# K S - V summed on TensorE and read by ScalarE in an attention's last chunks, low parts of the first weights on VectorE

## The chip, the core and the metric

One NeuronCore of a Trainium2 chip runs the whole program. The metric is device time in microseconds of one execution; lower is better.

## What is computed

The output of a delta-rule attention is the input of a rotating mixer, and that mixer's output goes through a normalised two-layer network. Shapes: batch 4, 8 heads, 768 tokens, head width 48, so 384 channels. Cut to what matters:

```python
for t in range(S):                                   # attention, per batch and head
    y[:, :, t] = q_t @ state
    v_old = k_t @ state                              # k_t is normalised
    state += beta_t * outer(k_t, v_t - v_old)
theta = x @ w_theta                                  # mixer on x = the attention's y
y = w_tok_r @ (x * cos(theta)) + w_tok_i @ (x * sin(theta))
u = x + y
u = u + relu(u @ w_ch)
xn = (u - mean) / sqrt(var + 1e-6) * g_ln            # network
out = u + relu(xn @ w_ch1) @ w_ch2
```

## The kernel before, in words

**Attention.** The tokens are cut into 24 chunks of 32. All 32 pairs of batch and head run side by side, as two halves h = 0, 1 of 16. Within a chunk the recurrence is solved with an inverse of a 32x32 triangle (PT, made for four chunks at a time on VectorE and POOL, the last one during chunk 18), so that only the state S runs from chunk to chunk. The loop body (L604 to L650) issues, in this order, for chunk c: R(0, c), which multiplies K with the state (L437, eight matmuls into the first half of the PSUM tile RW[0]) and has VectorE form Rs = V - K S (L440); S(1, c-1), the state update of the other half from the chunk before (L466) with two ScalarE copies into bds (L471); W(0, c), which multiplies PT with Rs (L452, second half of RW[0]) and has ScalarE copy the result into bdw in four pieces (L458); the output matmuls of chunk c-1 (L492), their ScalarE copy ys (L498) and four stores on SP's queue (L501); R(1, c); S(0, c); W(1, c); and the matmuls of q with the state (L481). Every engine starts its instructions in the order in which the program issues them to it. V is scaled by POOL two chunks ahead (L145). After the loop the last chunk's output matmuls follow (L651).

**Work of the next stage inside the attention.** At three places of each chunk, late(c, 0), late(c, 1) and late(c, 2), the program issues work of the mixer (L1149 to L1189). late(18, 2) sets constants (halfpi and magic, POOL memsets at L843 and L845, in memory that the inverse has just given back) and starts the weights' loads; late(20, 2) and late(21, 2) transpose the first two pieces of x (L870) and take them out as a high part xh (ScalarE, L879), a low part xl (VectorE, L883) and a copy u (ScalarE, L885, after xl); theta is a matmul (L897); angles make kk (ScalarE, L906) and nf (VectorE, L907); sines and cosines are ScalarE functions into the tile zf (L914, L915, L922), of which there is one buffer; turn multiplies zf with x on VectorE (L931) and copies it as the high part zh on ScalarE (L932); rest makes the low part zl on VectorE (L938).

**Weights.** Weights arrive as 64-bit floats in halves of 128x768 elements; there are two buffers for the raw halves, and the load of the next one waits on SP's queue until one is free. Weights.step, called at every late place from (19, 1) on, alternates between two actions. One finishes a half (parts, L800: ScalarE casts the high part at L813, then the low part is formed at L820, on POOL for the first two weights w0 and w1 and on VectorE from w2 on) and starts the next one (magnitude, L777, and clamp, L787 and L788, on VectorE), and then issues the next load. The other (low, L797 and L798, on VectorE) completes the bits and frees the raw buffer. The theta weights come first, then w0, w1 and w2 in two halves each. After the attention the same steps are issued by pump (L724), where the magnitude is ScalarE's (L781).

**Mixing.** Then 24 steps follow (L1239 to L1283), each with 36 matmuls (L957) that need one weight's high and low part and one zh and zl. Later stages are matmuls too (L1012, L1071, L1090).

Of the kernel before, what the change touches and what calls it, by code (L numbers as in the profile page):

```python
# [6 lines left out]
F32 = mybir.dt.float32  # L7
# [3 lines left out]
AF = mybir.ActivationFunctionType  # L11
ALU = mybir.AluOpType
# [4 lines left out]
NC = 24  # L17
# [72 lines left out]
        return False  # L90


def attention(ctx, tc, kq, ktok, vin, betai, maskin, x, psa, late=None):

    nc = tc.nc
    cst = ctx.enter_context(tc.tile_pool(name="a_cst", bufs=1))
# [334 lines left out]
    def R(h, c):  # L431
        if c == 0:
            return V[0][:, 4 * h:4 * h + 4, :]
        b = bds[h][c % 2]
        for g in range(2):
            for r in range(4):
                nc.tensor.matmul(RW[h][32 * r:32 * r + 32, 0, 2 * g:2 * g + 2, :], KQ[c][:, 0, 2 * h + g, r, :],  # L437
                                 b[:, 4 * g + r, :, :], start=True, stop=True)
        Rs = p2.tile([128, 4, D], F32, name=f"Rs{h}")
        nc.vector.tensor_tensor(out=Rs, in0=V[c][:, 4 * h:4 * h + 4, :], in1=RW[h][:, 0, :, :], op=ALU.subtract)  # L440
        return Rs

# [161 lines left out]
    for c in range(1, NC):  # L604
        s = c // 4
        step[0] = c
        load_kq(c + 11)
        load_v(c + 5)
        scale_v(c + 2)
        load_kt(c + 2)  # L610
        wa, wm, wq = Work(), Work(), Work()
        for n in {1: (9, 10), 2: (11, 12)}.get(c, (c + 10,)):
            if n < NC:
                a_work(wa, n)
        ym_work(wm, c - 1)
        yq_work(wq, c)
        R0 = R(0, c)
        budget = 2.3 if c >= 14 else 3.08
        if c % 4 == 1 and c > 1 and s + 1 < NS:
            while ("tg", s + 1) not in done:  # L620
                dv.step()
        dv.run(budget)
        if late:
            late(c, 0)
        wa.run((0.0 if c == 2 else 0.42) * wa.left())
        S(1, c - 1)
        W(0, c, R0)
        norms()
        wm.flush()
        R1 = R(1, c)  # L630
        dv.run(budget)
        if late:
            late(c, 1)
        if (c % 4 == 3 and s + 1 < NS) or c == 18:
            while s + 1 not in PT:
                if not dv.step():
                    norms()
        wa.flush()
        S(0, c)
        W(1, c, R1)  # L640
        norms()
        wq.flush()
        if c == 13:
            soon.close()
        if c == 18:
            mid.close()
        if c == 19:
            early.close()
        if late:
            late(c, 2)  # L650
    ym_work(pe, NC - 1)  # L651
    pe.flush()


def attn_inputs(q, k, v, beta):
# [173 lines left out]
class Mixer:  # L829
# [21 lines left out]
    def load_w(self, s, wtok, pool, wts, w=None):  # L851
        if pool:
            w = [pool.tile([128, 4, C], F32R, name=f"w{s}_{i}") for i in range(2)]
        self.W[s] = w
        for q in range(2):
            r = slice(2 * q, 2 * q + 2)
            wts.add(("w", s, q), wtok[s, q], lambda r=r: self.W[s][0][:, r], lambda r=r: self.W[s][1][:, r],
                    split=0 if s > 1 else None)

    def trans(self, i):  # L860

# [59 lines left out]
        zf = self.ZF  # L921
        nc.scalar.activation(out=zf[:, 0], in_=kk, func=AF.Sin, scale=-TWO_PI, bias=self.halfpi)  # L922

    def turn(self, i):
        nc = self.nc
        b, s = MIX[i]
        xs = self.x[s][:, b]
        zf = self.ZF
        zh = self.zp.tile([128, 2, C], F32R, name="zh")
        zl = self.zp.tile([128, 2, C], F32R, name="zl")  # L930
        nc.vector.tensor_tensor(out=zf, in0=zf, in1=bc(xs.unsqueeze(1), [128, 2, C]), op=ALU.mult)  # L931
        nc.scalar.copy(out=zh, in_=zf)  # L932
        self.Z[i] = zh, zl
        self.ZF2 = zf

# [189 lines left out]
def build(tc, a):  # L1125
# [8 lines left out]
    with tc.manual_schedule(), outer:  # L1134
# [10 lines left out]
        psa = outer.enter_context(tc.tile_pool(name="ps_a", bufs=2, space=PSUM, **R))  # L1145
        mx = Mixer(nc, x, psa, ident, uT)
        wts = Weights(nc, None, wide)

        def late(c, k):  # L1149
            if (c, k) == (13, 2):  # L1150
# [2 lines left out]
            if (c, k) == (18, 2):  # L1153
                nc.gpsimd.memset(ones.bitcast(F32), 1.0)
                nc.scalar.copy(out=ones, in_=ones.bitcast(F32))
                wts.st = ph1.enter_context(tc.tile_pool(name="st", bufs=1, **R))
                mx.load_theta(ph1, tc, a["wth"], wts)
                wts.load()
                nc.sync.dma_start(out=ident, in_=a["ident"])
                nc.sync.dma_start(out=g, in_=a["g"])  # L1160
            if (c, k) == (19, 2):
                mx.open(ph1, tc)
# [2 lines left out]
                wts.load()  # L1165
            if c > 19 or (c, k) == (19, 1):
                wts.step()
            if (c, k) == (16, 2):
                nc.scalar.activation(out=warm, in_=warm, func=AF.Sin)
            if (c, k) == (20, 2):  # L1170
# [7 lines left out]
            if (c, k) == (22, 2):  # L1178
                mx.cosines()
            if (c, k) == (22, 2):  # L1180
                mx.turn(0)
                mx.rest(0)
            if (c, k) == (23, 0):
                mx.theta(1)
                mx.angles(1)
            if (c, k) == (23, 1):
                mx.sines()
            if (c, k) == (23, 2):
                mx.cosines()  # L1189

        with ExitStack() as att:
            attention(att, tc, a["kq"], a["ktok"], a["vin"], a["betai"], a["mask"], x, psa, late)
        lp = outer.enter_context(tc.tile_pool(name="left", bufs=1))
        for b in range(1, 4):
            uT.append(lp.tile([128, KB, T], F32, name=f"u{b}"))
# [152 lines left out]
```

## Time and profile before

| | us |
|---|---|
| median of 3 runs | 785.29 |
| lowest of the runs | 783.65 |
| the profiled execution, in all | 786.73 |
| its span on the core | 784.8 |

| engine | busy us | share of the span |
|---|---|---|
| TensorE, matmul (PE) | 709.4 | 90% |
| TensorE, weight load (PEld) | 655.4 | 84% |
| VectorE (DVE) | 517.8 | 66% |
| ScalarE (ACT) | 356.9 | 45% |
| GpSimd (POOL) | 213.2 | 27% |

The profile's other views are used below: the chain that ended last, the busy time by stretch, groups of instructions by line with the idle time before them and what ended it, and the timeline of an engine. A releaser is the instruction whose semaphore came last. PEclk is the TensorE clock that was granted, as a share of full speed.

### The profile page before, as it was taken

The page shows a single profiled execution, that of the slowest core. Times are in us where ns is not written, and L with a number is a line of the kernel's source. Part 1 is how long each engine was busy: PE and PEld are TensorE (multiplying, and loading weights), DVE is VectorE, ACT ScalarE, POOL GpSimd, SP SyncE. Part 2 cuts the span into 40 slices and gives each one's busy share as a digit, 9 for nine tenths or more (in the row PEclk, how much of TensorE's full clock was granted, in tenths as well). Part 3 has the DMA queues.
Part 4 walks back from the last instruction along what each step waited for, and adds up shares of the span by engine and source line. Part 5 has one row for each costly group of instructions (what it writes and reads, how often), then busy time and mean ns, then how long its engine had stood idle before and what let it go on. Part 6 is the DMA issues. An engine that isn't in the chain of part 4 may idle for free.

```text
span 784.8 us, 18939 instructions
## 1 busy us (share of the span) xinstructions
PE 709.4 (90%) x7955; PEld 655.4 (84%) x7956; DVE 517.8 (66%) x875; ACT 356.9 (45%) x785; POOL 213.2 (27%) x234
## 2 busy tenths in 40 slices
PE   4577887777778999999997999999999999999997
PEld 3455555554468999999997999999999999999997
DVE  7987989986877888888876755435353534444342
ACT  2276776786775766654444433131322222131211
POOL 5854755744020001211111433113131221121120
PEclk8699999999989999999999999999999999999999
DMA  8975767234444223532432220000000000000000
GB/s 250 248 225 172 201 189 214 83 86 137 153 152 162 88 75 101 165 118 80 121 101 81 101 81 5 26 1 31 1 31 1 31 1 30 1 9 24 1 31 30
DMA packets 29716, 71.39 MB, mean 91 GB/s; under 512 B 4928, under 2 KB 17472, under 8 KB 29632
## 3 DMA queue, kind: packets, MB, share of 16 engines
q1 hardware_dynamic: 29632, 70.19, 29.0%
q8 instruction: 62, 1.02, 0.6%
q14 instruction: 22, 0.18, 0.1%
HBM read 56.02 MB, written 9.44 MB: 83 GB/s over the span
## 4 chain that ended last, share of the span: by engine, by line
PE 64%; DVE 15%; DMA 6%; ACT 6%; issue 5%; POOL 2%; SPq 1%; ACTq 0%; DVEq 0%; POOLq 0%
PE ph L1071 19%; PE acc L1090 19%; PE y L957 11%; PE pc L1012 5%; PE pth L897 3%; DMA bdk<-kq 3%; DVE prod L369 2%; ACT bdw L458 2%; DMA raw<-wtok 2%; PE py L492 1%; PE S L466 1%; PE pa L174 1%; DVE t L797 1%; PE RW L452 1%; DVE Ti L378 1%
## 5 line engine op out<-in xcount | busy, mean ns | idle before, releaser
L957 PE MATMUL y<-w,zh 128*128 128x384 f32 x576 | 154.8, 342 | 3.4 <-DVE u L966 2.4
L1090 PE MATMUL acc<-hh,f 128*128 128x384 f32 x576 | 147.0, 336 | 0.0
L1076 DVE SCALAR_TENSOR_TENSOR hl<-ph,hh 128x384 fp32r<-128x384 f32 x96 | 52.4, 553 | 114.5 <-ACT hh L1075 114.5
L1075 ACT ACTIVATE hh<-ph 128x384 fp32r<-128x384 f32 x96 | 46.7, 491 | 163.0 <-PE ph L1071 163.0
L1071 PE MATMUL ph<-xh,f 128*128 128x384 f32 x576 | 116.4, 337 | 0.4 <-DVE u L966 0.4
L957 PEld LDWEIGHTS y<-w,zh 128*128 128x128 f32 x576 | 105.8, 190 | 4.2 <-issue 2.7
L1090 PEld LDWEIGHTS acc<-hh,f 128*128 128x128 f32 x576 | 104.5, 188 | 0.0
L1071 PEld LDWEIGHTS ph<-xh,f 128*128 128x128 f32 x576 | 101.9, 188 | 0.7 <-issue 0.7
L957 PE MATMUL y<-w,zl 128*128 128x384 f32 x288 | 97.7, 339 | 2.4 <-DVE zl L938 2.4
L1090 PE MATMUL acc<-hl,f 128*128 128x384 f32 x288 | 96.9, 336 | 0.0
L1071 PE MATMUL ph<-xl,f 128*128 128x384 f32 x288 | 65.7, 336 | 0.0
L458 ACT COPY bdw<-RW 32x192 f32<-32x192 f32 x192 | 59.5, 310 | 13.6 <-PE RW L452 11.0
L957 PEld LDWEIGHTS y<-w,zl 128*128 128x128 f32 x288 | 54.6, 190 | 3.0 <-DVE zl L938 3.0
L471 ACT COPY bds<-S 48x384 f32<-48x384 f32 x92 | 43.5, 472 | 29.0 <-PE S L466 27.4
L466 PE MATMUL S<-bdw,ktt 128*48 128x192 f32 x368 | 42.0, 351 | 14.4 <-ACT bdw L458 14.3
L1090 PEld LDWEIGHTS acc<-hl,f 128*128 128x128 f32 x288 | 54.0, 188 | 0.0
L806 POOL TENSOR_TENSOR t<-t,g 128x384 f32<-128x384 f32 x12 | 15.3, 1279 | 135.3 <-DVE t L798 123.3
L1071 PEld LDWEIGHTS ph<-xl,f 128*128 128x128 f32 x288 | 51.6, 188 | 0.0
L452 PEld LDWEIGHTS RW<-Rs,pt 32*32 32x32 f32 x1472 | 19.8, 109 | 36.6 <-DVE Rs L440 28.5
L452 PE MATMUL RW<-Rs,pt 32*32 32x48 f32 x1472 | 26.4, 210 | 21.4 <-DVE Rs L440 21.0
L466 PEld LDWEIGHTS S<-bdw,ktt 128*48 128x48 f32 x368 | 20.8, 128 | 28.7 <-ACT bdw L458 22.2
L1100 POOL TENSOR_TENSOR o<-u,o 128x384 f32<-128x384 f32 x21 | 20.8, 1017 | 85.0 <-DVE o L1099 85.0
(165 smaller groups left out, 1305.8 us busy)
## 6 DMA issues: line engine op xcount, KB each, us to landing
kqt<-kq SPq DMA_DIRECT2D x20, 512.0 KB, 5.5
raw<-wtok SPq DMA_DIRECT2D x12, 768.0 KB, 4.7
raw<-wff SPq DMA_DIRECT2D x12, 768.0 KB, 4.9
bdk<-kq SPq DMA_DIRECT2D x40, 192.0 KB, 4.0
vt<-vin SPq DMA_DIRECT2D x24, 192.0 KB, 4.9
ktt<-ktok SPq DMA_DIRECT2D x24, 192.0 KB, 4.6
x<-ys SPq DMA_DIRECT2D x96, 48.0 KB, 2.5
flat<-t SPq DMA_DIRECT2D x12, 384.0 KB, 5.5
```

The costliest lines, as they stand in the source:

```text
L452: nc.tensor.matmul(RW[h][rr, 1, j, :], PT[c // 4][rr, m0 + j, :], Rs[rr, j, :], start=True, stop=True)
L458: nc.scalar.copy(out=b[rr, :, r, :], in_=RW[h][rr, 1, :, :])
L466: nc.tensor.matmul(S_ps[h][64 * e:64 * e + D, g, :], KT[c][:, 2 * h + g, e, :], b[:, 2 * g + e, :, :], start=(c == 0 and g == 0), stop=Tru ...
L471: nc.scalar.copy(out=n[ee, :, e, :], in_=S_ps[h][ee, :, :].rearrange("p g (r d) -> p (g r) d", r=4))
L897: nc.tensor.matmul(ps, l[:, k], self.tw[w][:, k], start=(n == 0), stop=(n == 8))
L957: nc.tensor.matmul(self.Y[q], l[:, ri, 128 * k:128 * k + 128], self.W[s][w][:, 2 * ri + h], start=(first and w == ri == 0 and l is zh), st ...
L1012: nc.tensor.matmul(ps, self.wc[w][:, k, 128 * e:128 * e + 128], r[:, k], start=(n == 0), stop=(n == 8))
L1071: nc.tensor.matmul(ps, w[:, 0, 128 * k:128 * k + 128], r[:, k], start=(n == 0), stop=(n == 8))
L1075: nc.scalar.activation(out=hh, in_=ps, func=AF.Relu)
L1076: nc.vector.scalar_tensor_tensor(out=hl, in0=ps, scalar=0.0, in1=hh.bitcast(F32), op0=ALU.max, op1=ALU.subtract)
L1090: nc.tensor.matmul(self.ACC[j][e], w[:, 1, 128 * e:128 * e + 128], r, start=(f == 0 and n == 0), stop=(f == NF - 1 and n == 2))
L1100: (nc.vector if j == NJ - 1 else nc.gpsimd).tensor_tensor(out=o, in0=u[:, e], in1=o, op=ALU.subtract)
```

## The change

From chunk 19 on, R first issues one matmul of V with a matrix "minus" (the negated identity) into the first half of RW, the eight K S matmuls add to it, and ScalarE takes the sum out with the factor -1; VectorE's subtraction is left out there. minus is made by POOL in late(18, 2) from ident, whose load moves from late(18, 2) to late(16, 0). The low parts of all weights are formed by VectorE (split = 0), those of w0 and w1 too. The first z is made in three pieces: the product at (22, 2), its high part zh at (23, 0), its low part zl at (23, 1) ahead of the sines. The last chunk's output matmuls, their copy and their stores are issued ahead of late(23, 2) instead of after it.

```diff
--- before.py
+++ after.py
@@ -90,7 +90,10 @@
         return False
 
 
-def attention(ctx, tc, kq, ktok, vin, betai, maskin, x, psa, late=None):
+LAST = 19
+
+
+def attention(ctx, tc, kq, ktok, vin, betai, maskin, x, psa, minus, late=None):
 
     nc = tc.nc
     cst = ctx.enter_context(tc.tile_pool(name="a_cst", bufs=1))
@@ -432,11 +435,16 @@
         if c == 0:
             return V[0][:, 4 * h:4 * h + 4, :]
         b = bds[h][c % 2]
+        if c >= LAST:
+            nc.tensor.matmul(RW[h][:, 0, :, :], minus[0], V[c][:, 4 * h:4 * h + 4, :], start=True, stop=True)
         for g in range(2):
             for r in range(4):
                 nc.tensor.matmul(RW[h][32 * r:32 * r + 32, 0, 2 * g:2 * g + 2, :], KQ[c][:, 0, 2 * h + g, r, :],
-                                 b[:, 4 * g + r, :, :], start=True, stop=True)
+                                 b[:, 4 * g + r, :, :], start=c < LAST, stop=True, skip_group_check=c >= LAST)
         Rs = p2.tile([128, 4, D], F32, name=f"Rs{h}")
+        if c >= LAST:
+            nc.scalar.activation(out=Rs, in_=RW[h][:, 0, :, :], func=AF.Copy, scale=-1.0)
+            return Rs
         nc.vector.tensor_tensor(out=Rs, in0=V[c][:, 4 * h:4 * h + 4, :], in1=RW[h][:, 0, :, :], op=ALU.subtract)
         return Rs
 
@@ -646,10 +654,11 @@
             mid.close()
         if c == 19:
             early.close()
+        if c == NC - 1:
+            ym_work(pe, c)
+            pe.flush()
         if late:
             late(c, 2)
-    ym_work(pe, NC - 1)
-    pe.flush()
 
 
 def attn_inputs(q, k, v, beta):
@@ -855,7 +864,7 @@
         for q in range(2):
             r = slice(2 * q, 2 * q + 2)
             wts.add(("w", s, q), wtok[s, q], lambda r=r: self.W[s][0][:, r], lambda r=r: self.W[s][1][:, r],
-                    split=0 if s > 1 else None)
+                    split=0)
 
     def trans(self, i):
 
@@ -921,7 +930,13 @@
         zf = self.ZF
         nc.scalar.activation(out=zf[:, 0], in_=kk, func=AF.Sin, scale=-TWO_PI, bias=self.halfpi)
 
-    def turn(self, i):
+    def turn(self, i, part=None):
+        if part != 1:
+            self.turn_(i)
+        if part != 0:
+            self.nc.scalar.copy(out=self.Z[i][0], in_=self.ZF2)
+
+    def turn_(self, i):
         nc = self.nc
         b, s = MIX[i]
         xs = self.x[s][:, b]
@@ -929,7 +944,6 @@
         zh = self.zp.tile([128, 2, C], F32R, name="zh")
         zl = self.zp.tile([128, 2, C], F32R, name="zl")
         nc.vector.tensor_tensor(out=zf, in0=zf, in1=bc(xs.unsqueeze(1), [128, 2, C]), op=ALU.mult)
-        nc.scalar.copy(out=zh, in_=zf)
         self.Z[i] = zh, zl
         self.ZF2 = zf
 
@@ -1145,6 +1159,7 @@
         psa = outer.enter_context(tc.tile_pool(name="ps_a", bufs=2, space=PSUM, **R))
         mx = Mixer(nc, x, psa, ident, uT)
         wts = Weights(nc, None, wide)
+        minus = []
 
         def late(c, k):
             if (c, k) == (13, 2):
@@ -1156,7 +1171,6 @@
                 wts.st = ph1.enter_context(tc.tile_pool(name="st", bufs=1, **R))
                 mx.load_theta(ph1, tc, a["wth"], wts)
                 wts.load()
-                nc.sync.dma_start(out=ident, in_=a["ident"])
                 nc.sync.dma_start(out=g, in_=a["g"])
             if (c, k) == (19, 2):
                 mx.open(ph1, tc)
@@ -1165,6 +1179,11 @@
                 wts.load()
             if c > 19 or (c, k) == (19, 1):
                 wts.step()
+            if (c, k) == (16, 0):
+                nc.sync.dma_start(out=ident, in_=a["ident"])
+            if (c, k) == (18, 2):
+                minus.append(ph1.enter_context(tc.tile_pool(name="minus", bufs=1, **R)).tile([128, 128], F32, name="minus"))
+                nc.gpsimd.tensor_scalar(out=minus[0], in0=ident, scalar1=-1.0, scalar2=None, op0=ALU.mult)
             if (c, k) == (16, 2):
                 nc.scalar.activation(out=warm, in_=warm, func=AF.Sin)
             if (c, k) == (20, 2):
@@ -1178,18 +1197,19 @@
             if (c, k) == (22, 2):
                 mx.cosines()
             if (c, k) == (22, 2):
-                mx.turn(0)
-                mx.rest(0)
+                mx.turn(0, 0)
             if (c, k) == (23, 0):
+                mx.turn(0, 1)
                 mx.theta(1)
                 mx.angles(1)
             if (c, k) == (23, 1):
+                mx.rest(0)
                 mx.sines()
             if (c, k) == (23, 2):
                 mx.cosines()
 
         with ExitStack() as att:
-            attention(att, tc, a["kq"], a["ktok"], a["vin"], a["betai"], a["mask"], x, psa, late)
+            attention(att, tc, a["kq"], a["ktok"], a["vin"], a["betai"], a["mask"], x, psa, minus, late)
         lp = outer.enter_context(tc.tile_pool(name="left", bufs=1))
         for b in range(1, 4):
             uT.append(lp.tile([128, KB, T], F32, name=f"u{b}"))
```

## Rows read from the trace of the kernel before

**Rows 1.** The chain that ended last: start us, length us, what.
```profile
236.71 4.17 DMA raw<-wtok
...
250.38 4.78 PE y L957 x17
...
265.26 6.27 PE y L957 x36
```

**Rows 2.** Busy by stretch: length, PE, PEld, DVE, ACT, POOL, PEclk, DMA share, GB/s.
```profile
184.00:230.00 46.00, 32.66 (x816) 22.88 (x816) 34.41 (x52) 34.26 (x84) 8.72 (x11) 0.90 0.48 155
...
258.00:345.00 87.00, 87.00 (x512) 86.64 (x511) 74.62 (x109) 55.28 (x98) 8.41 (x6) 1.00 0.33 109
...
186.00:188.00 2.00, 1.69 (x48) 1.21 (x52) 0.26 (x2) 1.04 (x4) 1.89 (x5) 0.62 0.34 86
```

**Rows 3.** Groups, 199 to 230 us: busy, mean ns | idle before, releaser.
```profile
L458 ACT COPY bdw<-RW 32x192 f32<-32x192 f32 x26 | 8.1, 310 | 1.1 <-PE RW L452 0.8
L820 POOL TENSOR_TENSOR w<-t,w 128x768 fp32r<-128x768 f32 x4 | 7.6, 1900 | 35.3 <-ACT w L813 35.3
...
L798 DVE SCALAR_TENSOR_TENSOR t<-raw,t 128x768 uint32<-128x768 uint32 x4 | 3.8, 958 | 0.1
...
L452 PE MATMUL RW<-Rs,pt 32*32 32x48 f32 x192 | 3.6, 216 | 7.5 <-DVE Rs L440 7.5
...
L440 DVE TENSOR_TENSOR Rs<-vt,RW 128x192 f32<-128x192 f32 x6 | 2.1, 345 | 0.0
```

**Rows 4.** Timeline at chunk 19, POOL, TensorE, ScalarE: start, length, what [idle, releaser].
```profile
186.11 0.10 POOL L843 MEMSET halfpi<- 128x1 f32 x1 [1.97 <-DVE pt L425]
...
186.31 0.77 PE L452 MATMUL RW<-Rs,pt 32*32 32x48 f32 x32 [1.18 <-DVE Rs L440]
...
188.29 0.87 PE L437 MATMUL RW<-bds,kqt 128*32 128x96 f32 x16
189.09 1.23 PE L466 MATMUL S<-bdw,ktt 128*48 128x192 f32 x8
...
190.42 0.97 ACT L471 COPY bds<-S 48x384 f32<-48x384 f32 x2 [1.31 <-PE S L466]
```

**Rows 5.** Timeline of ScalarE, chunks 20 to 23.
```profile
197.12 0.96 ACT L471 COPY bds<-S 48x384 f32<-48x384 f32 x2
...
211.92 0.48 ACT L885 COPY u<-pt 128x384 f32<-128x384 f32 x1 [1.91 <-DVE xl L883]
...
222.51 0.94 ACT L471 COPY bds<-S 48x384 f32<-48x384 f32 x2
```

**Rows 6.** Timeline of POOL, then of VectorE, where first weights are split.
```profile
208.69 1.84 POOL L820 TENSOR_TENSOR w<-t,w 128x768 fp32r<-128x768 f32 x1 [20.09 <-ACT w L813]
...
208.78 2.18 DVE L788 TENSOR_SCALAR t<-t 128x768 uint32<-128x768 uint32 x1
...
214.20 0.55 DVE L777 TENSOR_SCALAR t<-raw 128x768 uint32<-128x768 uint32 x1
...
215.98 2.55 DVE L797 SCALAR_TENSOR_TENSOR t<-raw,t 128x768 uint32<-128x768 uint32 x1
...
239.65 0.95 DVE L820 TENSOR_TENSOR w<-t,w 128x768 fp32r<-128x768 f32 x1
```

**Rows 7.** Timeline at the attention's end: ScalarE, VectorE, SP's queue.
```profile
226.06 0.52 ACT L914 ACTIVATE zf<-nf 128x384 f32<-128x384 f32 x1 [0.81 <-DVE nf L907]
...
227.28 1.27 ACT L458 COPY bdw<-RW 32x192 f32<-32x192 f32 x4 [0.28 <-PE RW L452]
228.58 0.83 ACT L813 CAST w<-t 128x768 fp32r<-128x768 f32 x1
...
230.15 0.48 ACT L498 COPY ys<-py 128x384 f32<-128x384 f32 x1 [0.22 <-PE py L492]
...
231.48 0.56 DVE L883 TENSOR_TENSOR xl<-pt,xh 128x384 fp32r<-128x384 f32 x1 [1.67 <-ACT xh L879]
...
230.65 2.41 SPq L501 DMA_DIRECT2D x<-ys  x4
```

## What the change is expected to do

> **What bounds the kernel now.** I read the span from its end backwards. In the chain that ended last the reader is to see that the long mixing stage is not reached by TensorE's own work: before its third step stands a load of raw weights at 236.71, whose buffer a VectorE step had to free, and only at 250.38 does TensorE go on [rows 1]. The busy time by stretch gives the boundary: from 258 to 345 us TensorE is busy 87.00 of 87 us, so whatever shifts that stage shifts the end by as much; from 184 to 230 it is busy 32.66 of 46, with VectorE (34.41) and ScalarE (34.26) both nearly as full [rows 2]. The change lies wholly in that second stretch and just behind it. The waits there are grouped by line [rows 3]: W's matmuls (L452) stood 7.5 us for Rs, which VectorE makes behind the weights in its queue. That is what can be gained. The two other rows to look at are POOL's low parts (L820), which stood 35.3 us for ScalarE's high parts without anyone caring, and ScalarE's bdw copies (L458), which hardly wait (1.1 us in 26): ScalarE's order paces the attention here.
>
> I write x.0, x.1, x.2 for the three places late(x, k) of chunk x, "hi" for ScalarE's high part (L813), "lo" for the low part, "low" for L797 with L798, "magnitude" for L777, L787 and L788. All times are forward walks through the queues in program order, with the durations of the rows.
>
> **Chunk 19: minus is late.** V's matmul is now the first thing of chunk 19 on TensorE, and it needs minus. minus is made by POOL behind the memset of halfpi, which began at 186.11 after standing 1.97 us for VectorE's transpose of the last inverse [rows 4], because its pool takes that memory. The new POOL instruction on 128x128 is in no row; it lies between the 0.10 of a 128x1 memset [rows 4] and the 1.84 of a 128x768 tensor_tensor [rows 6], by length 0.39. So minus is there at 186.6. Queued behind V's matmul on TensorE are K S of head half 0, S(1,18), W, and behind those on ScalarE Rs, the two bds and the four bdw copies. Before, K S and S(1,18) ran ahead of the transpose, for nothing. TensorE will have stood some 3 us; before it stood 1.18 us [rows 4] and the granted clock then fell to 0.62 over 186 to 188 [rows 2], so I take that level (1.2 GHz) rows: V 0.5 (two of the eight S records at 1.23, 0.3, and a weight load), K S 0.87, S 1.23 [rows 4]: 189.2. Then bds 0.97 [rows 4], bdw 1.27 [rows 7], S(0,19) and its 0.9 to the next bds: 192.4 where before it was 190.42 [rows 4]. **+2.0.** At the upper level V, K S and S take half, 1.3 less, of which some 0.5 returns because before was slow there too: bound +1.2; slow to the end of S(0,19): bound +2.4.
>
> A rule bears on the clock here: the Trainium skill, TensorE: Matmul & The Clock Gate, What's actually happening, says that the throttled state is the default and that activity releases it. By that rule a longer stand can only make the low level likelier; by it the term is the +2.0 I took.
>
> **Rs on ScalarE.** Ten instructions of 192 elements leave VectorE (0.345 each) and come to ScalarE at 0.31, the price of bdw with 192 elements [rows 3]; the ten V matmuls after the first lie in TensorE's waits for bdw and cost nothing while ScalarE paces (without that cover 0.3 each, 3 us). Where ScalarE had a gap, Rs hides; where bds followed without one, as at 197.12 [rows 5], Rs shows. Walking on: chunk 20 +0.3, chunk 21 +0.3 and then -0.45 (W no longer waits for VectorE), chunk 22 +0.65: **+0.8** (bounds 0, all hidden, and +3.1, none). Most of the 7.5 us of waits is not recovered, because Rs now stands behind ScalarE's copies of u (L885), which themselves wait for VectorE's xl: the row at 211.92 stood 1.91 us for it [rows 5], and Rs of chunk 22 comes after it.
>
> **Low parts on VectorE.** Four lo leave POOL (1.9 us each, [rows 3]) and cost VectorE 0.95 each, 0.87 to the next instruction [rows 6]. Against that two stretches go: L788 at 208.78 took 2.18 us while POOL ran its lo from 208.69, and L797 at 215.98 took 2.55 instead of 0.96 [rows 3, 6]; 3.2 us in all. By work alone VectorE comes out even. But lo waits for hi, and behind it in VectorE's queue stand the next magnitude, nf and xl; before, POOL did that waiting. At 21.2 hi comes after the bdw copies of chunk 21, at 210.6, while VectorE is done at 209.4: 1.2 us stand, then lo 0.87, magnitude 1.78 (214.20 to 215.98, [rows 6]), nf and xl 0.46 each, and u starts at 214.4 against 211.92 [rows 5]. At 22.1 hi stands behind ys and Rs of chunk 22 on ScalarE; VectorE waits from 216.2 to 218.9. low ends at 223.4, and hi, zh and kk of 23.0 follow, so that bds of chunk 23 starts at 225.6 against 222.51 [rows 5]: +3.1, of which this step has **+0.3** after its 3.2 us of gain (bounds: -3.2 if VectorE never stands, and +1.7, which is three lo, 2.6, and stands of 3.9, less 3.2 and the 1.6 that six Rs leave free).
>
> **z in pieces.** zl (rest) now comes behind chunk 23's second low on VectorE. There lo (225.2), magnitude (227.0), nf, low (229.4) and zl (0.9) end at 230.4 to 230.5. sines(1) writes the single zf buffer that zl still reads, so it waits; and behind sines on ScalarE stand the last four bdw. Before, sines began at 226.06 and bdw at 227.28 [rows 7]. ScalarE alone would be free at 228.6 (225.6 + bds 0.97 + bdw 1.27 + ys 0.4 + Rs 0.3), so it stands 1.9 us; sines and its Abs take 0.9, bdw starts at 231.4: +4.1, **+1.0** from this step (bounds 0, if low runs earlier, and +1.9).
>
> **ym ahead of late(23, 2).** On ScalarE ys, which waits for TensorE's last py, now stands before hi and the cosine; before, hi ran at 228.58 and ys at 230.15 [rows 7]. Counted from the end of py: ys 0.4, hi 0.75, lo 0.87, magnitude 1.78, then xl: 3.9 where it was 1.4 (231.48, [rows 7]). +2.5, less 0.3 to 0.4 that py itself catches up: **+2.1** (bounds 0, if mixing does not wait for xl, and +2.5). The load of the eighth raw unit (second half of w2) moves behind four stores of x on SP's queue, ahead of which it stood (they took 2.41 from 230.65, [rows 7]), to about 237, landing 4.2 later [rows 1] at 241.2; it is needed when low of the seventh ends at 242.8, so it is covered by 1.6 us. From xl on the chain is the old one: zf, zh, zl, low, the raw load, y. TensorE goes on at 256.6 instead of 250.38 [rows 1]. The earlier ident load is covered: SP is idle there.
>
> **Sum.** 2.0 + 0.8 + 0.3 + 1.0 + 2.1 = 6.2 us; all lower bounds together give -2.0, all upper ones +11.6. Span 784.8 + 6.2 = 791.0. The profiled execution took 786.73 in all, 1.4 over the median of the runs, 785.29; the time to be measured is that of the median: 785.3 + 6.2 = 791.5.
>
> **Rivals.** *Faster: VectorE's queue lets go.* If the 7.5 us of waits for Rs [rows 3] vanish and nothing takes their place, with minus late (+2.0) and the tail (+2.1) unchanged, it is 785.3 - 3.4 = 782. For it: VectorE loses 3.4 us of Rs and 3.2 us of stretches. Against it: bdw waits so little that ScalarE has no room. It decides at S(1,22): if bds of chunk 23 starts before 220, this one holds. The Trainium skill, SBUF — State Buffer, Who interferes with whom, says that a VectorE instruction with two SBUF inputs or in a two-port mode and a GpSimd instruction that reads SBUF exclude each other for its whole length. By that rule up to four times 1.9 us of lock would go, and the gain would be larger, 7.6 where I count 3.2; the trace agrees with the mechanism in two of the four (2.18 instead of 0.56 us), in the others VectorE was waiting anyway.
>
> *About as before.* VectorE's waits for hi fall where ScalarE paces anyway, and xl of trans(2) is not what mixing waits for: then only minus is left, +2.0, 787. For it: by work alone VectorE comes out even. Against it: the chain of rows 1 runs through xl.
>
> *Slower still: the clock.* TensorE stands in chunk 23 for zl and again for bdw; if the low level lasts through the first mixing step, its 36 matmuls take twice their 6.27 us [rows 1]: up to +6 more, 797. Against it: mixing waits for the chain, not for TensorE.
>
> **Chances.** The forecast 0.60 (788 to 796), about as before 0.18, faster 0.12, the clock 0.10. The range 783 to 798 holds all but the far ends of the last two. A measurement of this kernel tells 2%, 15.7 us, from no change; none of the cases reaches 769.6, and only the clock together with the forecast's upper bounds comes near 801. So faster 0.02, same 0.94, slower 0.04.
>
> **What would show it.** V's matmul of chunk 19 at 186.6 behind POOL's minus, and bds at 192.4 instead of 190.42; u at 214.4 with VectorE idle for ScalarE before lo; sines waiting for zl and bdw of chunk 23 at about 231; VectorE idle 4 to 5 us before the lo at the end; TensorE gap-free from about 264. Wrong, if bds of chunk 23 starts before 222.5, if sines does not wait for zl, or if xl of trans(2) comes within 2 us of the last py.

## The result, and the profile after

| | before | after |
|---|---|---|
| median, us | 785.23 | 794.12 |
| lowest of the runs | 783.65 | 792.71 |
| the profiled execution, in all | 786.73 | 792.71 |
| its span | 784.8 | 790.7 |

The ratio is 1.0119, with a 95% interval of 1.0093 to 1.0146: slower by 1.2%, 8.9 us by the medians. That is less than the 2% from which a comparison here calls a kernel slower. The time lies in the forecast case (788 to 796, likeliest 791.5). One of the four runs of the kernel before took 1723.75 us; it is counted in the median above (785.17 without it) and left out of the ratio.

First the boundary that the prediction started from. This is the busy time by stretch of the kernel after, with the columns of [rows 2]:

```profile
184.00:230.00 46.00, 38.38 (x820) 25.08 (x824) 26.84 (x41) 32.94 (x84) 2.50 (x4) 0.87 0.44 144
...
264.00:345.00 81.00, 80.81 (x473) 79.78 (x473) 70.06 (x102) 51.30 (x93) 8.06 (x6) 1.00 0.35 108
```

From 264 us on TensorE is busy 80.81 of 81 us, so the end still moves with the moment at which mixing gets going. In the stretch of the attention VectorE was busy 26.84 us for 34.41 and POOL 2.50 for 8.72 [rows 2]; only a part of that is less work, the rest is work that came later. The page's first line has what the whole span saved, VectorE 3.8 us (517.8 before) and POOL 7.2 (213.2):

```profile
PE 719.0 (91%) x7975; PEld 659.8 (83%) x7976; DVE 514.0 (65%) x869; ACT 358.1 (45%) x795; POOL 206.0 (26%) x231
```

The chain that ended last (start, length, what) still runs through a raw load ahead of the third zl. The load starts 6.9 us later than in [rows 1], the zl 6.8 us later than before, where it started at 249.38:

```profile
243.56 4.14 DMA raw<-wtok
...
256.15 0.95 DVE zl L952
```

So one number carries the comparison: the time from the start of VectorE's last inverse transpose (the last work before chunk 19's weights; 184.04 us before, 181.46 after) to the start of the third zl (the low part that the third mixing step needs). From there to the end of the span every one of the fourteen profiled kernels took 534.3 to 535.6 us. This stretch is 65.34 us before and 74.69 after: **+9.35**, beside 8.9 in the medians. (The spans differ by 5.9 only, because in the profiled execution of after the transpose happened to start 2.6 us earlier and what follows the third zl took 0.9 us less. Over the fourteen kernels it started between 179.6 and 189.5, ahead of nearly all that the edits touch.)

Where the stretch grew, in the marks that the prediction named, each as us after the start of that transpose. The column "forecast" is the mark of the prediction less 184.04; for sines it is worked out from the 230.5 at which the prediction has zl end, for xl from the sum of 6.2:

| mark | before | forecast | after |
|---|---|---|---|
| bds that S(0,19) releases | 6.38 | 8.36 | 9.95 |
| u of 21.2 | 27.88 | 30.36 | 32.06 |
| bds of chunk 23 | 38.47 | 41.56 | 44.73 |
| sines of 23.1 | 42.02 | 46.5 | 49.42 |
| last bdw | 43.24 | 47.36 | 50.26 |
| xl of trans(2) | 47.44 | 53.6 | 56.89 |
| third zl | 65.34 | 71.54 (+6.2) | 74.69 |

Three stretches show where the 9.35 us came from. The first is chunk 19, TensorE's timeline of after (start, length, engine, line, what, in brackets the idle time before and its releaser):

```profile
184.18 1.01 PE L439 MATMUL RW<-vt,minus 128*128 128x192 f32 x2 [3.65 <-POOL minus L1186]
185.12 0.87 PE L442 MATMUL RW<-bds,kqt 128*32 128x96 f32 x16
185.92 1.52 PE L474 MATMUL S<-bdw,ktt 128*48 128x192 f32 x8
187.37 0.86 PE L460 MATMUL RW<-Rs,pt 32*32 32x48 f32 x32
189.46 0.59 PE L439 MATMUL RW<-vt,minus 128*128 128x192 f32 x2
189.98 0.54 PE L442 MATMUL RW<-bds,kqt 128*32 128x96 f32 x16
190.45 0.86 PE L474 MATMUL S<-bdw,ktt 128*48 128x192 f32 x8
...
214.28 0.86 PE L460 MATMUL RW<-Rs,pt 32*32 32x48 f32 x32 [3.01 <-ACT Rs L446]
215.07 1.51 PE L500 MATMUL py<-bdw,mt 128*32 128x192 f32 x16
216.51 1.01 PE L439 MATMUL RW<-vt,minus 128*128 128x192 f32 x2
```

V's matmul stood 3.65 us for minus. The same instructions appear in two lengths: V 1.01 and then 0.59, S 1.52 and then 0.86. The busy time by stretch (columns as above) has the clock beside it, the lower of its two levels (0.50 is 1.2 GHz) after the stand, and again after the second stand of 3.01 us at 214.28:

```profile
186.00:188.00 2.00, 2.00 (x40) 1.21 (x40) 0.00 (x0) 0.79 (x2) 0.50 (x1) 0.50 0.81 307
...
190.00:192.00 2.00, 2.00 (x72) 1.43 (x75) 1.74 (x2) 1.22 (x4) 0.00 (x0) 1.00 0.10 25
...
214.00:216.00 2.00, 1.72 (x44) 1.27 (x48) 1.31 (x2) 1.81 (x6) 0.00 (x0) 0.50 0.01 3
```

What minus itself waited for stands in POOL's timeline of after; the transpose of the last inverse on VectorE ended at 183.44, and minus is made behind it:

```profile
183.50 0.10 POOL L852 MEMSET halfpi<- 128x1 f32 x1 [1.93 <-DVE pt L428]
...
183.60 0.53 POOL L1186 TENSOR_SCALAR minus<-ident 128x128 f32<-128x128 f32 x1
```

The second and third stretch are ScalarE's timeline of after in chunks 22 and 23, where u waits for xl, Rs behind u, and sines for zl:

```profile
213.52 0.48 ACT L894 COPY u<-pt 128x384 f32<-128x384 f32 x1 [2.64 <-DVE xl L892]
213.89 0.34 ACT L446 ACTIVATE Rs<-RW 128x192 f32<-128x192 f32 x1
...
218.39 0.33 ACT L446 ACTIVATE Rs<-RW 128x192 f32<-128x192 f32 x1 [1.26 <-PE RW L442]
...
230.88 0.52 ACT L923 ACTIVATE zf<-nf 128x384 f32<-128x384 f32 x1 [1.71 <-DVE zl L952]
...
234.57 0.48 ACT L506 COPY ys<-py 128x384 f32<-128x384 f32 x1 [1.59 <-PE py L500]
234.94 0.83 ACT L822 CAST w<-t 128x768 fp32r<-128x768 f32 x1
```

The waits of after from 181 to 262 us (who waits for whom: us in total, times, longest) add them up:

```profile
DVE w L829 <- ACT w L822: 10.1, 3, 5.0
...
ACT u L894 <- DVE xl L892: 6.0, 3, 2.6
PE RW L460 <- ACT Rs L446: 6.0, 3, 3.0
```

The groups of the stretch from 199 to 230, with the columns of [rows 3]:

```profile
L466 ACT COPY bdw<-RW 32x192 f32<-32x192 f32 x24 | 7.4, 310 | 0.5 <-PE RW L460 0.2
...
L460 PE MATMUL RW<-Rs,pt 32*32 32x48 f32 x192 | 3.7, 221 | 6.0 <-ACT Rs L446 6.0
L829 DVE TENSOR_TENSOR w<-t,w 128x768 fp32r<-128x768 f32 x3 | 2.9, 959 | 5.1 <-ACT w L822 5.0
...
L446 ACT ACTIVATE Rs<-RW 128x192 f32<-128x192 f32 x6 | 2.0, 335 | 1.3 <-PE RW L442 1.3
```

Before, W's matmuls stood 7.5 us for VectorE's Rs [rows 3]; now they stand 6.0 us for ScalarE's Rs, and ScalarE stands 6.0 us for xl in its copies of u. VectorE stands 10.1 us for ScalarE's high parts ahead of its own low parts; on POOL that wait (35.3 us, [rows 3]) held up nobody.

### The profile page after: what moved, and what is told of

It reads as the page before. It is cut to its first block, busy times and chain, and to the rows that moved or that the text cites. A ratio compares the mean times of both kernels' runs of the same rounds, so it can differ in the third digit from the quotient of the medians.

```text
span 790.7 us, 18964 instructions
## 1 busy us (share of the span) xinstructions
PE 719.0 (91%) x7975; PEld 659.8 (83%) x7976; DVE 514.0 (65%) x869; ACT 358.1 (45%) x795; POOL 206.0 (26%) x231
## 4 chain that ended last, share of the span: by engine, by line
PE 54%; DVE 12%; ACT 4%; issue 3%; DMA 2%; POOL 0%; SPq 0%; ACTq 0%; DVEq 0%; POOLq 0%
PE ph L1085 19%; PE acc L1104 19%; PE y L971 7%; PE pc L1026 5%; PE pth L906 2%; DVE t L807 2%; DVE t L806 2%; DVE zl L952 1%; DVE zf L946 1%; DVE t L797 1%; DMA raw<-wtok 1%; DVE t L796 1%; DVE w L829 1%; DMA flat<-t 1%; ACT zf L931 1%
## 5 line engine op out<-in xcount | busy, mean ns | idle before, releaser
L474 PE MATMUL S<-bdw,ktt 128*48 128x192 f32 x368 | 44.0, 365 | 13.2 <-ACT bdw L466 13.1
L177 PE MATMUL pa<-bdk,kqt 128*32 128x128 f32 x640 | 29.7, 327 | 12.1 <-DMA kqt<-kq 5.8
```

The lines of the kernel that those rows point to most:

```text
L177: nc.tensor.matmul(hold[0][32 * r:32 * r + 32, g, :, :].rearrange("p e (k i) -> p e k i", k=2), KQ[c][:, 0, g, r, :], bdk[c % 2][:, :, :, ...
L474: nc.tensor.matmul(S_ps[h][64 * e:64 * e + D, g, :], KT[c][:, 2 * h + g, e, :], b[:, 2 * g + e, :, :], start=(c == 0 and g == 0), stop=Tru ...
```

## The experiments

Every kernel below computes the whole result. "Stretch" is the time from the last inverse transpose to the third zl; it comes from one profiled execution each, while the ratio comes from several runs beside the kernel before on the same chip. Whether the clock fell at chunk 19 differs between executions: before, the bds that S(0,19) releases came at 6.38 with the clock down; in the executions of lo alone and ym alone it did not fall, and the same mark came at 5.16 and 5.18. Their stretches are about 1.2 us short for that reason. Six kernels have the late minus and run the same code up to this mark; it came at 9.22 to 9.26 in four of them, at 9.95 in after and at 10.19 in e11. Chunk 22 differs between executions in the same way, as e5 shows below.

| kernel | stretch | less before | median | ratio, 95% interval |
|---|---|---|---|---|
| before | 65.34 | | 785.2 to 786.4 | |
| after | 74.69 | +9.35 | 794.12 | 1.0119, 1.0093 to 1.0146 |
| e1 K S - V alone | 69.41 | +4.07 | 790.22 | 1.0059, 1.0032 to 1.0086 |
| e2 lo alone | 65.13 | -0.21 | 786.21 | 1.0010, 0.9991 to 1.0029 |
| e3 z in pieces alone | 68.62 | +3.28 | 787.24 | 1.0024, 0.9998 to 1.0051 |
| e4 ym alone | 65.46 | +0.12 | 785.56 | 1.0006, 0.9986 to 1.0025 |
| e5 after, minus early | 67.58 | +2.24 | 789.89 | 1.0058, 1.0027 to 1.0088 |
| e6 after, lo undone | 70.36 | +5.02 | 792.88 | 1.0097, 1.0065 to 1.0130 |
| e7 after, z undone | 72.07 | +6.73 | 794.49 | 1.0116, 1.0072 to 1.0161 |
| e8 after, ym undone | 71.24 | +5.90 | 793.48 | 1.0101, 1.0041 to 1.0162 |
| e9 K S - V alone, minus early | 64.54 | -0.80 | 785.43 | 0.9996, 0.9974 to 1.0019 |
| e10 lo alone, behind magnitude | 66.22 | +0.88 | 787.47 | 1.0013, 0.9987 to 1.0039 |
| e11 after, u ahead of xl | 71.14 | +5.80 | 795.14 | 1.0114, 1.0084 to 1.0145 |
| e12 e9 with u ahead of xl | 62.49 | -2.85 | 783.14 | 0.9957, 0.9940 to 0.9974 |

### One part at a time

**e1: K S - V alone.** The kernel after, with the low parts, z and ym as before.

```diff
-                    split=0)
+                    split=0 if s > 1 else None)
...
-                mx.turn(0, 0)
+                mx.turn(0)
+                mx.rest(0)
...
+    ym_work(pe, NC - 1)
+    pe.flush()
```

> Only the sum on TensorE with Rs on ScalarE (and the earlier load of ident); low parts, z and the last output matmuls as before. Counted from the start of VectorE's last transpose of the inverse to the third zl (65.3 us before, 74.7 after the whole change). Theory A (the wait for minus holds all of chunk 19, and Rs only moves the queue it stands in): +4 to +5, about 789.5 us; V's matmul starts when POOL's minus ends and the second bds after it comes 3.6 us later than before. Rival B (VectorE's queue lets go): the 7.5 us of waits for Rs vanish against 3.6, so -2 to -4, about 782.

The stretch grew by 4.07 and the time by 0.59%, 4.6 us: theory A, and this part is half of the loss. The stand is there as in after, in TensorE's timeline of e1, with V still at its shorter length and S at its longer one. The mark of S(0,19)'s bds came 2.9 us later than before, where 3.6 was expected:

```profile
185.44 0.59 PE L439 MATMUL RW<-vt,minus 128*128 128x192 f32 x2 [3.67 <-POOL minus L1180]
...
186.43 1.52 PE L474 MATMUL S<-bdw,ktt 128*48 128x192 f32 x8
```

**e2: low parts alone.** The kernel before with one line changed.

```diff
-                    split=0 if s > 1 else None)
+                    split=0)
```

> Only the low parts of w0 and w1 on VectorE. Theory A (VectorE now stands for ScalarE's high part with the next half behind it): three or four stands of VectorE before the low part, 1 to 3 us each, which eat the 3.2 us that the two stretched instructions give back: 0 to +3, about 786.5. Rival B (the lock of VectorE against POOL was the cost): the two instructions of 2.2 and 2.5 us fall to 0.6 and 1.0 and the time falls by 2 to 3, about 782.5.

1.0010, nothing that can be told from nothing. VectorE's timeline of e2 has the stands for ScalarE's high part, shorter than in after:

```profile
212.83 0.96 DVE L820 TENSOR_TENSOR w<-t,w 128x768 fp32r<-128x768 f32 x1 [0.97 <-ACT w L813]
220.30 0.96 DVE L820 TENSOR_TENSOR w<-t,w 128x768 fp32r<-128x768 f32 x1 [1.53 <-ACT w L813]
...
234.30 0.96 DVE L820 TENSOR_TENSOR w<-t,w 128x768 fp32r<-128x768 f32 x1 [1.29 <-ACT w L813]
```

**e3: z in pieces alone.** The kernel before with turn split in two and its parts at (22, 2), (23, 0) and (23, 1).

```diff
-                mx.turn(0)
-                mx.rest(0)
+                mx.turn(0, 0)
             if (c, k) == (23, 0):
+                mx.turn(0, 1)
...
             if (c, k) == (23, 1):
+                mx.rest(0)
                 mx.sines()
```

> Only z in three pieces. Theory A: the sines of chunk 23 wait for zl, which comes behind the second low part of that chunk: sines some 3 us later than before, the last bdw 2.5 us later, +2 to +3, about 787.8. Rival B (VectorE no longer stands for zh, so Rs of chunk 23 comes 1.8 us earlier and carries on): -1, about 784.

The stretch grew by 3.28, the time by 0.24% (1.9 us, with an interval from -0.2 to +4.0). ScalarE's timeline of e3 shows the new wait: sines stands for zl, because both use the one buffer of zf.

```profile
228.42 0.52 ACT L914 ACTIVATE zf<-nf 128x384 f32<-128x384 f32 x1 [4.45 <-DVE zl L943]
```

**e4: ym alone.** The kernel before with the last chunk's output ahead of late(23, 2).

```diff
+        if c == NC - 1:
+            ym_work(pe, c)
+            pe.flush()
         if late:
             late(c, 2)
-    ym_work(pe, NC - 1)
-    pe.flush()
```

> Only the last output matmuls ahead of the last late work. Theory A: ScalarE's high part and cosine stand behind the copy that waits for TensorE, and the eighth raw load behind the stores of x: xl of the third transposition 0.9 us later, +1 to +2, about 786.5. Rival B: hidden, 0, 785.2.

1.0006: by itself this edit is not seen in the time. The four parts alone add up to 0.99% (7.8 us), the whole is 1.19%; the difference of 1.5 us is within the intervals.

### What the late minus costs

**e5: after, with minus made in chunk 17.** Its memory is taken at (13, 2), so that it does not wait for what the inverse gives back.

```diff
             if (c, k) == (13, 2):
...
+                minus.append(ph1.enter_context(tc.tile_pool(name="minus", bufs=1, **R)).tile([128, 128], F32, name="minus"))
...
-            if (c, k) == (18, 2):
-                minus.append(ph1.enter_context(tc.tile_pool(name="minus", bufs=1, **R)).tile([128, 128], F32, name="minus"))
+            if (c, k) == (17, 1):
                 nc.gpsimd.tensor_scalar(out=minus[0], in0=ident, scalar1=-1.0, scalar2=None, op0=ALU.mult)
```

> The whole change, but minus is made by POOL in chunk 17 in memory that was free since chunk 13, so chunk 19 waits for nothing. Theory A: the 3.6 us of chunk 19 come back and, since K S no longer stands behind VectorE's transpose, up to 1.2 more: the third zl 70 to 71 us after the transpose instead of 74.7, about 790. Rival (the wait only moves to the next queue, ScalarE and VectorE pace the rest anyway): less than 1.5 us come back, about 793.

1.0058 against 1.0119 for after: half of the loss goes, 4.8 us by the ratios and 7.1 us in the stretch, more than theory A expected (67.58 for 70 to 71). The mark of S(0,19)'s bds came 5.48 us earlier. The other 1.6 us lie in chunk 22, where W's matmuls stood 2.66 us for Rs and yet the granted clock was 1.00 from 206 to 216 us. TensorE's timeline of e5:

```profile
211.32 0.54 PE L460 MATMUL RW<-Rs,pt 32*32 32x48 f32 x32 [2.66 <-ACT Rs L446]
...
212.58 0.59 PE L439 MATMUL RW<-vt,minus 128*128 128x192 f32 x2
```

From u of 21.2 to bds of chunk 23 it takes 11.05 us in e5, 11.05 in e8 as well, where W stood 2.94 us and the granted clock stayed at 1.00 too, and 12.67 in after, where it fell to 0.50. So the second fall of the clock is worth 1.6 us, and a stand of nearly 3 us does not bring it every time.

**e9** makes the same edit in e1.

> The kernel before with only the sum on TensorE and Rs on ScalarE, and minus made in chunk 17. Theory A (what this part costs is the wait for minus and the clock that falls with it; Rs itself is neither gain nor loss): 65.3 us to the third zl as before, within 1, 785 to 786.5 us. Rival B (ScalarE paces, so ten Rs on it cost by themselves): +2 to +3, 788. Rival C (VectorE's queue lets go once minus is no matter): -2 to -4, 782.

0.9996 against 1.0059 for e1: 4.9 us, and no loss is left, theory A. At chunk 19 TensorE's timeline of e9 has neither the stand nor the long records:

```profile
182.50 0.59 PE L439 MATMUL RW<-vt,minus 128*128 128x192 f32 x2
...
183.73 0.86 PE L474 MATMUL S<-bdw,ktt 128*48 128x192 f32 x8 [0.17 <-ACT bdw L466]
```

Two pairs of kernels thus give the lateness of minus the same price, 4.8 and 4.9 us, each known to some 3 us by the intervals of its two ratios. At chunk 19 the mark of S(0,19)'s bds is 4.47 in both e5 and e9, 6.38 before and 9.95 in after. So the part would have gained 1.9 us there, since K S - V no longer hangs on VectorE while it makes the last transpose; 1.2 of these are the clock, which fell there in before, and 0.7 remain beside e2 and e4, where it did not. Being late the part lost 3.6.

### One part undone

**e6: after, low parts of w0 and w1 on POOL again.**

```diff
-                    split=0)
+                    split=0 if s > 1 else None)
```

> The whole change, but the low parts of w0 and w1 on POOL again. Theory A: VectorE's stands before the low part (10.1 us in the trace of after) go, and the stretches by POOL's lock (up to 1.6 each) return: -1 to -3, third zl at about 72.5, 792. Rival (the move was a gain by the lock): +1 to +2, 796.

**e7: after, first z whole at (22, 2) again.**

```diff
-                mx.turn(0, 0)
+                mx.turn(0)
+                mx.rest(0)
...
-                mx.turn(0, 1)
...
-                mx.rest(0)
```

> The whole change, but the first z whole at (22, 2). Theory A: sines of chunk 23 no longer wait 1.7 us for zl: -1.5 to -2.5, third zl at about 72.7, 792. Rival (the pieces keep ScalarE free for Rs and bds in chunk 23): +1, 795.

**e8: after, last chunk's output behind late(23, 2) again.**

```diff
-        if c == NC - 1:
-            ym_work(pe, c)
-            pe.flush()
...
+    ym_work(pe, NC - 1)
+    pe.flush()
```

> The whole change, but the last output matmuls behind the last late work again. Theory A: high part and cosine run while TensorE makes py, and VectorE's 5.0 us stand shrinks: xl of the third transposition 2.4 us earlier, third zl at about 72.3, 791.8. Rival (mixing waits for something else): no change, 794.

The stretches shrank by 4.3, 2.6 and 3.5 us; the ratios fell by 0.22%, 0.03% and 0.18% (1.7, 0.2 and 1.4 us), none of which is larger than the intervals. The directions of e6 and e8 are those expected, their sizes are open, and for e7 the time shows no gain. In e7 1.8 us of the stretch lie between bds of chunk 23 and the last bdw, where they were expected. Of the 3.5 us of e8, 1.5 had come by the last bdw, ahead of the edit, where the clock of chunks 19 and 22 differed; that leaves 1.9 for the edit, 2.4 were expected. A stretch is one execution, in which the clock fell or held by its own chance, so where a stretch and a ratio of many runs differ, the ratio decides.

The last lines of these kernels settle a smaller point, the edits lo and ym at the attention's end. From the start of the last ys to xl of trans(2) it takes 1.33 us before [rows 7], 1.83 in e2 (lo alone), 2.13 in e4 (ym alone) and 3.78 in after (both): the two add 0.50 and 0.80 alone and 2.45 together. VectorE's timeline of after:

```profile
235.81 0.96 DVE L829 TENSOR_TENSOR w<-t,w 128x768 fp32r<-128x768 f32 x1 [5.03 <-ACT w L822]
...
238.35 0.55 DVE L892 TENSOR_TENSOR xl<-pt,xh 128x384 fp32r<-128x384 f32 x1
```

Ahead of xl VectorE has lo and a magnitude, and lo waits for the high part that ym has pushed behind ys. With lo on POOL (e4) VectorE is early and stands 2.46 us for xh; with ym behind (e8) this stand is 3.08 us instead of 5.03, as VectorE's timeline of e8 has it:

```profile
230.44 0.96 DVE L828 TENSOR_TENSOR w<-t,w 128x768 fp32r<-128x768 f32 x1 [3.08 <-ACT w L821]
```

### Is VectorE's time worth anything?

**e10: low parts on VectorE, issued behind the next magnitude.** This takes the stand for the high part away and keeps POOL out of VectorE's way.

```diff
-        self.finish()
+        lows = [self.parts(*u) for u in self.two]
+        self.two = []
         if self.loaded:
             self.one.append(self.magnitude(*self.loaded.pop(0), True))
+        for f in lows:
+            f()
...
-                    split=0 if s > 1 else None)
+                    split=0)
```

> The kernel before with the low parts of w0 and w1 on VectorE, each issued behind the next half's magnitude instead of ahead of it. Theory A (VectorE's stand for the high part was what ate the gain of the lock): no stands, no stretched instructions, third zl 2 to 3 us earlier, 783. Rival B (ScalarE paces the stretch, VectorE's time there is worth nothing): 0, 785.5.

1.0013. In VectorE's timeline of e10 lo no longer stands, and no instruction is stretched (before, one L788 took 2.18 us and one L797 2.55 [rows 6]):

```profile
215.23 0.56 DVE L791 TENSOR_SCALAR t<-t 128x768 uint32<-128x768 uint32 x1
215.70 0.95 DVE L823 TENSOR_TENSOR w<-t,w 128x768 fp32r<-128x768 f32 x1
216.57 0.95 DVE L800 SCALAR_TENSOR_TENSOR t<-raw,t 128x768 uint32<-128x768 uint32 x1
```

Yet W still stood 7.5 us for Rs in e10, 1.2 us less than before in the same window. The waits from 184 to 250 us, of e10 and then of before:

```profile
PE RW L452 <- DVE Rs L440: 7.5, 6, 2.4
```

```profile
PE RW L452 <- DVE Rs L440: 8.7, 6, 2.0
```

The edit also brought a stand of its own: the magnitude now goes ahead of the theta weights' low part too, and there VectorE stood 3.62 us for a raw load (1.34 before) with that low part and Rs behind it. VectorE's timeline of e10:

```profile
202.84 0.56 DVE L780 TENSOR_SCALAR t<-raw 128x768 uint32<-128x768 uint32 x1 [3.62 <-DMA raw<-wtok]
```

With this u of 21.2 came 1.4 us later than before (29.28 for 27.88); from there to the third zl e10 took 36.94 us, before 37.46. So the gain that I put against the cost of lo did not come in either kernel: in e2 the stands for the high part stood against it, in e10 the stand for the load. Theory B, that VectorE's time is worth nothing here, fits 1.0013 but is not shown by it; a gain of 3 us is outside the interval, one of 1 us is not. The Trainium skill, SBUF — State Buffer, Who interferes with whom, names the exclusion of VectorE and GpSimd that stretched the two instructions; the traces agree that it is there (2.18 against 0.56 us) and that it goes when POOL stops, but in e2 and e10 nothing was gained by its end.

### Who goes first, u or xl

**e11: after, with ScalarE's copy u issued ahead of VectorE's xl.** Both read the same PSUM tile. **e12** is the same edit in e9.

```diff
         self.transpose(i)
-        self.copies(i, 0)
+        self.copies(i)
```

> The whole change, but ScalarE copies u ahead of VectorE's xl, not behind it. Theory A (Rs of chunks 21 and 22 stands behind u, which stands 1.1, 2.6 and 2.3 us for xl): those stands go, W's longest wait for Rs of 3.0 us shrinks to about 0.5, third zl 2 to 4 us earlier than 74.7, about 791. Rival (something else on ScalarE holds Rs as long): no change, 794.

> The kernel before with only the sum on TensorE and Rs on ScalarE, minus made in chunk 17, and ScalarE's copy of u ahead of VectorE's xl. With minus early alone the time was that of before (785.4). Theory A (what keeps the moved Rs from paying is that it stands behind u, which stood 4.4 us for xl): third zl at 62 to 63 us after the transpose, 782.5 to 783.5 us, faster than both kernels by 0.3%. Rival (ScalarE paces the rest, the stands were slack): 64.5, 785.4, the same as before.

In e11 the stretch shrank by 3.6 us as expected, the time did not (1.0114 against 1.0119). The two ratios can be compared to some 0.4%, 3.2 us, so whether the edit gains anything here is open. In e12 both moved: 62.49 against 64.54 in e9, and the ratio fell from 0.9996 to 0.9957, by 0.39% give or take 0.28. A part of the 2.05 us in the stretch is the clock: in chunk 22 S took 1.52 us in e9, while in e12 the granted clock was 1.00 from 206 to 216. This is the one kernel that beats both, 783.14 us beside 786.35 before. ScalarE's timeline of e9 first, and then that of e12 at the same place:

```profile
209.98 0.48 ACT L893 COPY u<-pt 128x384 f32<-128x384 f32 x1 [2.72 <-DVE xl L891]
210.36 0.34 ACT L446 ACTIVATE Rs<-RW 128x192 f32<-128x192 f32 x1
```

```profile
207.98 0.49 ACT L893 COPY u<-pt 128x384 f32<-128x384 f32 x1
208.35 0.35 ACT L446 ACTIVATE Rs<-RW 128x192 f32<-128x192 f32 x1
```

With u standing no longer, Rs follows at once, and W's stands for Rs fall; the waits from 184 to 250 us, of e9 and then of e12:

```profile
PE RW L460 <- ACT Rs L446: 6.4, 4, 2.9
...
ACT u L893 <- DVE xl L891: 4.4, 3, 2.7
```

```profile
PE RW L460 <- ACT Rs L446: 4.5, 4, 1.6
```

## Why the prediction was right, and where its sizes were off

The forecast (slower by 6.2 us, to 791.5) had the sign and most of the mechanisms: the waits it named appeared with the releasers it named, at marks up to 3.3 us later than forecast. The median rose by 8.9. By its steps:

- **Minus is late: right mechanism, the term that was mis-sized.** I had +2.0 (bounds 1.2 to 2.4) at chunk 19; it measured +3.57 (and +2.84 to +3.81 in the five other kernels with the late minus). Minus came almost when I said, 2.67 us after the start of the transpose against 2.56. What came behind was longer. V's matmul I had at 0.5, from two of eight S records; it took 1.01 at the lower level and held K S up by 0.94. S took 1.52 for my 1.23. And I costed V once: with TensorE slow, ScalarE was no longer what paced chunk 19, so the second V matmul (0.52 to the next start) lay on the path too, and bds waited 0.49 for TensorE. My sentence that the other V matmuls "cost nothing while ScalarE paces" did not hold there. As a price of the lateness itself the term is larger still, 4.8 to 4.9 us (e5 against after, e9 against e1), because the part had a gain at chunk 19 that I did not see: without the stand the mark is at 4.47, 1.9 ahead of before, 1.2 of it the clock that fell in before.
- **Rs on ScalarE: +0.8 forecast, about right; what it did to the clock was missed.** e9 has this part without the late minus and comes to 0.9996. Behind the mark at chunk 19, from where the forecast counts this term, e9 took 60.07 us and before 58.96, 1.1 more in one execution each; the gain at that mark more than makes up for it. That Rs now stands behind u, which stands for xl, was right: u of 21.2 stood 2.64 us for xl (1.91 before, [rows 5]) and Rs of chunk 22 came right behind it. The consequence I missed: W's matmuls then stood 3.01 us at 214.28, and the clock fell a second time. py took 1.51 us, V 1.01, S 1.52, and the next Rs waited 1.26 for K S. That is half of why bds of chunk 23 came 6.26 late where I had 3.1; the other half, 1.57, is the error at chunk 19. In e5 and e8 the clock held after such a stand, so that it fell here was not certain either. e12 shows what the stand for xl is worth without the rest of the change: 0.39%, 3.1 us, give or take 2.2.
- **Low parts on VectorE: +0.3 forecast; +0.8 alone and 1.7 in company by the ratios, neither resolved.** The stand before lo at 21.2 was 0.90 for my 1.2, that of 22.1 4.13 for my 2.7: the high part stood behind the slow chunk 22. The credit of 3.2 us for stretches that go is not borne out: in e2 and e10 they are gone and the time is no shorter, in each beside a new stand of VectorE. Without the credit and with the longer stands the term would have been well above +0.3; that it measured so little fits VectorE standing mostly off the path, which no run shows by itself, so that the nearness of this term is luck.
- **z in pieces: right in the trace.** I had sines stand 1.9 us for zl and a net +1.0; it stood 1.71, and the last bdw was 0.76 later by comparison with bds of chunk 23. By the time it is not resolved: +1.9 us alone (e3, from -0.2 to +4.0), 0.2 in company (e7). In e3 the stand was 4.45: without the other delays ScalarE would have been there earlier. A second buffer for zf would tell how much of it is the buffer's; it wasn't tried.
- **ym ahead of late(23, 2): right as a sum, not as one edit's.** I had +2.5, less 0.4; from ys to xl it grew by 2.45. But alone the edit adds 0.80 (e4), and 1.0006 in the time: two thirds of it need lo on VectorE as well. The eighth raw load was not quite covered, as I had said it was: ScalarE's magnitude stood 1.46 us for it at 242.14, but ran on ahead of the third zl without showing there (+9.45 at xl, +9.35 at the third zl).
- **The rivals.** *VectorE's queue lets go* needed bds of chunk 23 before 220; it came at 226.19, and neither e2 nor e10, which free VectorE otherwise, gained anything; e12 gained, by another order of the same work. *About as before* needed VectorE's waits to be free; with xl 9.45 late they were not. *The clock* through the first mixing step did not happen: the step began at the lower level, its first matmuls taking 0.52 us instead of 0.33 (from 235.59), and by 237.13 they took 0.33. What cost time was the lower level in chunks 19 and 22, inside the attention, which is where I should have placed that rival.

In all, 8.9 is 6.2 plus some 1.6 at chunk 19 and some 1.6 in chunk 22, less what the medians do not show of the 9.35. In chunk 22 it is the lower clock level, by comparison with e5 and e8; at chunk 19 it is the lower level and the second V matmul, which no run takes apart.

## What to carry to other kernels

A constant that is made when memory comes free can be on the path from the first instruction that reads it: a new first operand in an in-order queue should be ready a chunk early, and here that alone was worth some 4.8 of 8.9 us. Before work is moved to relieve an engine, ask with one experiment whether that engine's time is worth anything at this place; here no way of freeing VectorE of its stretched instructions gained time, and each time it had to stand for its new neighbours instead. When two engines read one tile, let the one go first whose queue holds the next link of the chain: that order, and an early minus, made the only version that is faster than the kernel before; in e11, with the late minus, the same order gained nothing that the time shows.

## What the runs showed of the hardware

- After a stand of 3.65 us the granted clock was 0.50 in 186 to 188 and 1.00 again in 190 to 192; after one of 3.01 us it was 0.50 in 214 to 216. After stands of 2.66 us (e5) and 2.94 us (e8) at the same place it stayed at 1.00, and before it fell to 0.62 after one of 1.18 us (186 to 188), which e2 and e4 stood too without their S growing longer. At the lower level V took 1.01 instead of 0.59, S 1.52 instead of 0.86, py 1.51 instead of 0.86. At chunk 19 the mark of S(0,19)'s bds came 5.48 us later with the stand of 3.65 than without (9.95 against 4.47); in the five other kernels with the late minus it was 4.75 to 5.72, 1.3 to 1.6 times the stand.
- The last inverse transpose started between 179.6 and 189.5 us in the profiled executions of kernels that hardly differ until then, while medians of before agreed within 1.2 us on different chips (785.2 to 786.4). Two spans can't be subtracted; a stretch between two marks can, and even it moves with the clock, by 1.2 us at chunk 19 and by 1.6 in chunk 22.
- POOL's TENSOR_SCALAR on 128x128 took 0.53 us, for an estimate of 0.39 by length.
